# One bank's turn and one matmul's place at the change from block 1 to block 2 of a fused attention and PReLU feed-forward kernel

## The chip, the core and the metric

The kernel runs on one core of a Trainium2 chip. The metric is the device time of one execution in microseconds (us). The core's engines are named as the profile names them: PE (TensorE matmuls), PEld (its weight loads), DVE (VectorE), ACT (ScalarE), POOL (GpSimd), and SP, which only issues DMA transfers here.

## What is computed

Attention without softmax over 8 batches of 8 heads, 576 rows and 64 columns, a norm per row, and then a feed-forward layer with PReLU, all in the reference's own words:

```python
kv = np.einsum('bhsd,bhse->bhde', k, v)
out = np.einsum('bhsd,bhde->bhse', q, kv)
rms = np.sqrt(np.mean(out * out, axis=-1, keepdims=True) + 1e-06)
attn = out / rms * g_norm
x = attn.transpose(0, 2, 1, 3).reshape(4608, 512)
h = x @ w_in                                           # 512 -> 2048
g = np.maximum(h, 0.0) + alpha * np.minimum(h, 0.0)
y = g @ w_out                                          # 2048 -> 512
```

## The kernel before

The 4608 rows are worked off in 9 blocks of 512 (`w` = 0 to 8). A block's first product is cut into 16 **units** (`u` = 0 to 15), one for each 128 of the 2048 columns. A unit is `m1_group`: four matmuls of 128x512 into a PSUM bank `h_ps` (line 391), a relu of the negated bank by ACT into `m_sb` (line 398), and one operation by DVE that reads `m_sb` and the bank and writes the activation `gt` (line 402). The bank is free once that DVE operation has ended.

Which bank a unit gets is decided by `HPool` and `h_bank`: the turn `h_turn[0]` goes up by one, modulo the number of tags in `h_tags[0]`, and picks the tag. There are three tags, h0, h1 and h2, and block 1 starts with the turn at 0, so its units take h1, h2, h0, h1 and so on. In block 2, after unit 0, the list of tags becomes h1 and h2 alone (line 793), for all blocks that follow; h0 is from then on a bank of the second product.

The order of work on each engine is the order in which the program names it (a manual schedule): the loop over `w` and `u` at line 781 puts behind each unit's `m1_group` a share of other work. Each engine's instructions run in that order, and a tile's bank or buffer is taken again only when the last reader of its former contents is done.

The second product of block 0 is done plainly: 16 accumulating matmuls (`y_mm`, line 416) for each of four tiles of 128 rows. Three of these are finished before block 1. The fourth, `ys[3]`, is the **held-back tile**: it sits in the bank with tag "y", and its 16 matmuls are spread over the units of block 1. `Y3_AT[u]` gives, for each unit, the first matmul and the one after the last; those before 8 were done earlier. After the 16th, `y_out` copies the bank to SBUF with ACT (line 450) and `store_rows` issues its stores (line 427), on SP's queue.

From block 2 on, the second product of the block before is done with seven products in place of eight, on quarter blocks (`prod_mm`, line 546, matmuls of 128x256): seven matmuls behind each unit. Products 1 and 2 write the tile yX, which uses the bank with tag "y"; products 6, 7 and 4 write yY in h0; products 5 and 3 write yZ. The sums of `gt` that they need come from DVE (`s_sum`, lines 496 to 502). The attention of the next block (`step_kv` at line 327, `step_ot` at 349, `step_ssq` at 365 to 375) stands behind fixed units; `regroup_pair` (line 171, ACT) puts a part of k in order, and `dma_t` (line 317, SP) transposes q by DMA.

At the boundary the order on PE, behind `m1_group` of unit 14, is: matmul 14 of the held-back tile; unit 15; matmul 15 of the held-back tile; block 2's unit 0; seven matmuls of yX; unit 1; seven of yX; the first `step_kv` of batch 3.

Of the kernel before, what the change touches and what calls it, by code (L numbers as in the profile page):

```python
# [17 lines left out]
def kernel(  # L18
# [148 lines left out]
    def regroup(b, nm, h0, h1, eng=None):  # L167
        dst = bufs[b % NBUF][nm][:, 0:TPP, h0:h1, :].rearrange("p t h d -> p h t d")
        src = stages[b, nm][:, h0:h1, :, :]
        if eng is nc.scalar:  # L170
            nc.scalar.copy(out=dst, in_=src)
        else:
            (eng or nc.vector).tensor_copy(out=dst, in_=src)
# [6 lines left out]
    def load_gated(b):  # L180
        load_rem(b, "q")
        if b == B_NAT:
            load_q(b)
        load_rem(b, "k")
        load_main(b, "k")
        if b > B_NAT:
            load_q(b)
        load_rem(b, "v")
        load_main(b, "v")
# [8 lines left out]
    def regroup_pair(b, nm, j):  # L198
        regroup(b, nm, 2 * j, 2 * j + 2, nc.scalar)
# [112 lines left out]
    def dma_t(b):  # L312
        qt = attn_p.tile([P, NPAIR, S], FP16, name="qt_all")
        for t in range(NT):
            c0, c1 = t * P, min((t + 1) * P, S)
            src = stages[b, "q"][:, t] if t < TPP else buf_of(b, "q")[0:REM, TPP]
            nc.sync.dma_start_transpose(
                out=qt[:, :, c0:c1], in_=src.rearrange("p h d -> p (h d)"),
            )
        for j in range(NPAIR):  # L320
            qts[b, j] = qt[:, j, :]
# [59 lines left out]
    h_turn = [0]  # L381
# [25 lines left out]
    def m1_group(w, g, pool=None):  # L407
        h_ps = pool[0].tile([P, W], FP32, name="h_ps", tag=pool[1]) if pool else h_bank()
        m1_mm(h_ps, w, g, range(NC))
        m1_evac(h_ps, w, g)  # L410
# [4 lines left out]
    def y_mm(y, w, a, g):  # L415
        nc.tensor.matmul(  # L416
            out=y[:], lhsT=gt_cols(w, g, a * P, (a + 1) * P), rhs=w_out_blk(g),
            start=(g == 0), stop=(g == NF - 1),
        )
# [28 lines left out]
    def y_out(y, w, a):  # L448
        y_sb = ysb_p.tile([P, D_MODEL], FP32, name="y_sb")
        nc.scalar.copy(out=y_sb[:], in_=y[:])  # L450
        store_rows(w * W + a * P, y_sb[:], 0, D_MODEL)
# [37 lines left out]
    def s_sum(w, n, k):  # L489
        lo, hi = gts[w, k], gts[w, k + KQ]  # L490
        a11, a21 = lo[:, :, 0:HW], lo[:, :, HW:W]
        a12, a22 = hi[:, :, 0:HW], hi[:, :, HW:W]
        t = sum_p.tile([P, 2, HW], FP16, name=f"s{n}", tag=f"s{n}{k}", bufs=2 if n < 3 else 1)
        sums[w, n, k] = t
        if n == 1:
            nc.vector.tensor_add(out=t[:], in0=a21, in1=a22)
        elif n == 2:
            nc.vector.tensor_sub(out=t[:], in0=sums[w, 1, k][:], in1=a11)  # L498
        elif n == 3:
            nc.vector.tensor_sub(out=t[:], in0=a11, in1=a21)  # L500
        else:
            nc.vector.tensor_sub(out=t[:], in0=a12, in1=sums[w, 2, k][:])
# [20 lines left out]
    def prod_mm(w, n, i):  # L523
        a, c = divmod(i, NK)
        bank, fresh = y_bank(w, {1: "X", 2: "X", 6: "Y", 7: "Y", 4: "Y", 5: "Z", 3: "Z"}[n], a)
        cols = slice(a * P, (a + 1) * P)
        hi_cols = slice(HW + a * P, HW + (a + 1) * P)
        k, r = divmod(c, 2)
        if n == 1:
            lhs = gts[w, k][:, r, cols]  # L530
        elif n == 2:
            lhs = gts[w, k + KQ][:, r, cols]
        elif n == 4:
            lhs = gts[w, k + KQ][:, r, hi_cols]
        else:
            lhs = sums[w, {6: 2, 7: 3, 5: 1, 3: 4}[n], k][:, r, cols]
        q, rr = divmod(c, GW)
        if n == 1:
            rhs = w_out_sb[q][:, rr, 0:HC]
        elif n == 2:  # L540
            rhs = w_out_sb[q + WQ // 2][:, rr, 0:HC]
        elif n == 3:
            rhs = w_out_sb[q + WQ // 2][:, rr, HC:D_MODEL]
        else:
            rhs = wsum[{4: 4, 5: 1, 6: 2, 7: 3}[n]][:, c, :]
        nc.tensor.matmul(  # L546
            out=bank, lhsT=lhs, rhs=rhs, start=fresh, stop=(c == NK - 1), skip_group_check=True,
        )
# [12 lines left out]
    def y_read(w, what, subs=(0, 1)):  # L561
        if what == "p1":
            part[w, 1] = u_p.tile([P, 2, HC], FP32, name="p1")
            nc.scalar.copy(out=part[w, 1][:], in_=ybank[w, "X"][:])
            return
        if what in ("u2", "u3"):
            part[w, what] = u_p.tile([P, 2, HC], FP32, name=what)
            nc.vector.tensor_add(
                out=part[w, what][:], in0=ybank[w, "Y"][:], in1=part[w, 1][:]
            )  # L570
            return
        y_sb = ysb_p.tile([P, 2, HC], FP32, name="y_sb")
        if what == "c11":
            nc.scalar.copy(out=y_sb[:], in_=ybank[w, "X"][:])
        else:
            other = part[w, {"c21": 1, "c22": "u3", "c12": "u2"}[what]]
            if what == "c21":
                nc.vector.tensor_add(out=y_sb[:], in0=ybank[w, "Y"][:], in1=other[:])
            elif w < NW - 1:
                nc.vector.tensor_add(out=y_sb[:], in0=ybank[w, "Z"][:], in1=other[:])  # L580
            else:
                for a in subs:
                    nc.vector.tensor_add(
                        out=y_sb[:, a, :], in0=ybank[w, "Z", a][:], in1=other[:, a, :]
                    )
        quad_out(w, int(what[1]) - 1, int(what[2]) - 1, y_sb, subs)
# [160 lines left out]
    def unit_sums(w, u):  # L747
        for back, n, k in S_AT.get(u, ()):
            if 1 <= w + back < NW:
                s_sum(w + back, n, k)  # L750
# [13 lines left out]
    def attention(w, u):  # L764
        if w < NW:
            for what, j in (ATT_1 if w == 2 else ATT_AT).get(u, ()):
                if what == "t" and w >= B_NAT:
                    continue
                if w < B or what in ("ot", "ssq"):
                    if w == 2 and what in ("kv", "ssq"):  # L770
                        pool = Q_POOL if j % 2 == 0 else S_POOL
                        (step_kv if what == "kv" else step_ssq)(w, j, pool)
                    else:
                        ATT[what](w, j)

    REG_AT = {8 + 2 * j: (("k", j),) for j in range(NPAIR)}

    Y3_AT = [(8, 8), (8, 8), (8, 8), (8, 9), (9, 9), (9, 10), (10, 10), (10, 10), (10, 11), (11, 11), (11, 12), (12, 12), (12, 13), (13, 14), (14, 15), (15, 16)]
    REG_2 = {2 * j: (("k", j),) for j in range(NPAIR)}

    for w in range(1, NW):
        if w + 2 < B:
            load_gated(w + 2)
        for u in range(NF):
            m1_group(w, G_ORDER[u])
            if w > 1:
                unit_sums(w, u)
            if w == 1 and u == 2:
                regroup(2, "k", 0, H)
            if w == 1 and u == 3:  # L790
                dma_t(3)
            if w == 2 and u == 0:
                h_tags[0] = ("h1", "h2")
            if w > 2 and u == 0:
                y_read(w - 2, "c12")
            if w == 1:
                for i in range(*Y3_AT[u]):
                    y_mm(ys[3], 0, 3, i)
                    if i == NF - 1:
                        y_out(ys[3], 0, 3)  # L800
            else:
                for i in range(u * PER, (u + 1) * PER):
                    prod_mm(w - 1, *Y_LIST[i])
                for what in Y_READS.get(u, ()):
                    y_read(w - 1, what)
            attention(w + 1, u)
            if w == 1:
                for k in {5: (0,), 7: (1,)}.get(u, ()):
                    s_sum(1, 1, k)
                    s_sum(1, 2, k)  # L810
            if w + 2 < B:
                for nm, j in REG_AT.get(u, ()) if w > 1 else ():
                    regroup_pair(w + 2, nm, j)
                if u == 11 and w > 1:
                    dma_t(w + 2)
            if w == 2:
                for nm, j in REG_2.get(u, ()):
                    regroup_pair(3, nm, j)
                if u < 2:
                    s_sum(1, u + 1, 2)  # L820
# [48 lines left out]
```

## Time and profile before

| | |
|---|---|
| Time, median of 6 runs | 283.67 us (283.04 to 283.93) |
| Profiled execution, its own time | 283.51 us |
| Its span | 281.7 us |
| PE busy | 274.3 us (97%) |
| DVE, ACT busy | 219.7 us, 157.0 us |
| Granted PE clock | 1.00 |

The profile is one execution of the program, so its time differs a little from the median. Times in the views are counted from the start of its span, which is shorter than the device time by what lies around it. A view gives a start and a length; "x4" stands for four instructions of one form merged into one row, and what stands in brackets is the idle time of the engine ahead of the row and what ended it. Matmuls overlap: one of 128x512 is recorded with 379 ns, and the next starts 216 ns after it.

### The profile page before, as it was taken

How to read it: one execution, taken by the hardware profiler on the slowest of the kernel's cores; microseconds unless marked ns; L12 is line 12 of the kernel's file. 1: busy time of each engine (PE TensorE's matmuls, PEld its weight loads, DVE VectorE, ACT ScalarE, POOL GpSimd, SP SyncE). 2: the span in 40 equal slices, each digit the busy share in tenths (PEclk: the TensorE clock that was granted, in tenths of full speed). 3: DMA queues.
4: the chain of work that ended last, by engine and by line, in shares of the span. 5: the costliest groups of instructions: out<-in, count | busy, mean ns of one | idle time of the engine just before them, and what ended most of it. 6: DMA issues, size and time to landing. Idle time of an engine off the chain costs nothing.

```text
span 281.7 us, 4978 instructions
## 1 busy us (share of the span) xinstructions
PE 274.3 (97%) x1888; PEld 173.9 (62%) x1888; DVE 219.7 (78%) x418; ACT 157.0 (56%) x268; POOL 62.2 (22%) x85
## 2 busy tenths in 40 slices
PE   7899999999999999999999999999999999999995
PEld 3444444554666676666666666666666666666784
DVE  6569729898778878897879788878888788787872
ACT  3567447787667645664567466645554556443310
POOL 8744332740720036006300550000000000000000
PEclk9999999999999999999999999999999999999999
DMA  8999999999793369947973696330112011201223
GB/s 161 193 207 196 197 201 193 194 139 167 96 174 60 93 77 161 158 111 114 148 115 97 124 157 112 93 106 1 40 37 74 2 37 37 77 0 37 77 76 114
DMA packets 77628, 31.37 MB, mean 111 GB/s; under 512 B 45780, under 2 KB 77284, under 8 KB 77604
## 3 DMA queue, kind: packets, MB, share of 16 engines
q0 software_dynamic: 55600, 18.85, 59.0%
q1 hardware_dynamic: 21108, 11.25, 15.0%
q10 hardware_dynamic: 896, 0.95, 1.0%
q8 instruction: 15, 0.25, 0.4%
q14 instruction: 9, 0.07, 0.1%
HBM read 36.71 MB, written 9.44 MB: 164 GB/s over the span
## 4 chain that ended last, share of the span: by engine, by line
PE 84%; DMA 12%; issue 1%; POOL 1%; DVE 1%; ACT 0%; DVEq 0%; POOLq 0%
PE h_ps L391 39%; PE yY L546 15%; PE yZ L546 10%; PE yX L546 10%; DMA vst<-in_v_dram 5%; DMA w_in_sb<-in_moe_w_in_dram 5%; PE kv_ps L327 3%; PE ot_ps L349 3%; PE ssq_ps L365 2%; PE y L416 2%; DMA qst<-in_q_dram 2%; PE qt_ps L293 0%; POOL vst L136 0%; DVE xt L375 0%; DVE gt L402 0%
## 5 line engine op out<-in xcount | busy, mean ns | idle before, releaser
L391 PE MATMUL h_ps<-xt,w_in_sb 128*128 128x512 f16 x576 | 145.4, 379 | 0.7 <-DVE gt L402 0.5
L402 DVE SCALAR_TENSOR_TENSOR gt<-m_sb,beta_sb,h_ps 128x512 f16<-128x512 f32 x144 | 106.9, 746 | 40.8 <-ACT m_sb L398 39.0
L398 ACT ACTIVATE m_sb<-h_ps 128x512 f32<-128x512 f32 x144 | 86.0, 598 | 75.7 <-PE h_ps L391 61.0
L391 PEld LDWEIGHTS <-w_in_sb 128*128 128x128 f16 x576 | 54.8, 98 | 47.0 <-issue 1.7
L546 PEld LDWEIGHTS <-s 128*128 128x128 f16 x512 | 50.1, 98 | 19.3
L546 PEld LDWEIGHTS <-gt 128*128 128x128 f16 x384 | 37.6, 98 | 15.1 <-issue 0.4
L546 PE MATMUL yY<-wsum,s 128*128 128x256 f16 x256 | 36.3, 273 | 0.0
L546 PE MATMUL yX<-w_out_sb,gt 128*128 128x256 f16 x256 | 35.1, 273 | 0.1
L355 ACT ACTIVATE sq_sb<-ot_ps 128x512 f16<-128x512 f32 x36 | 21.3, 598 | 17.3 <-PE ot_ps L349 17.1
L367 ACT ACTIVATE rstd<-ssq_ps,eps_t 128x512 f32<-128x512 f32 x36 | 24.7, 690 | 9.7 <-PE ssq_ps L365 9.7
L375 DVE SCALAR_TENSOR_TENSOR xt<-ot_ps,g2col,rstd 128x512 f16<-128x512 f32 x36 | 26.5, 744 | 3.2 <-ACT rstd L367 3.2
L162 POOL DMA_DIRECT2D qsb<-in_q_dram x7 | 4.9, 699 | 78.7 <-DMA qt_all<-qsb 76.6
L153 POOL DMA_DIRECT2D qst<-in_q_dram x20 | 17.7, 916 | 1.9 <-DVE gt L402 1.9
L546 PE MATMUL yY<-wsum,gt 128*128 128x256 f16 x128 | 17.6, 273 | 0.0
L546 PE MATMUL yZ<-wsum,s 128*128 128x256 f16 x128 | 17.6, 273 | 0.0
L546 PE MATMUL yZ<-w_out_sb,s 128*128 128x256 f16 x128 | 17.6, 273 | 0.0
L416 PE MATMUL y<-w_out_sb,gt 128*128 128x512 f16 x64 | 17.0, 379 | 0.5 <-DMA w_out_sb<-in_moe_w_out_dram 0.5
L349 PE MATMUL ot_ps<-qt_all,kv_sb 128*128 128x512 f16 (+7 forms) x64 | 13.6, 286 | 0.4 <-DVE kv_sb L335 0.3
L327 PEld LDWEIGHTS <-ksb 128*128 128x128 f16 (+1 forms) x164 | 11.4, 98 | 4.2 <-DMA vst<-in_v_dram 1.1
L498 DVE TENSOR_TENSOR s<-s,gt 128x512 f16<-128x512 f16 x32 | 13.5, 421 | 0.5
L365 PE MATMUL ssq_ps<-sq_sb,mask 128*128 128x512 f16 x36 | 13.6, 379 | 0.2 <-ACT sq_sb L355 0.2
L335 DVE TENSOR_TENSOR kv_sb<-kv_ps,mask 128x128 f16<-128x128 f32 x32 | 9.1, 285 | 6.0 <-PE kv_ps L327 6.0
(66 smaller groups left out, 211.0 us busy)
## 6 DMA issues: line engine op xcount, KB each, us to landing
out_dram<-y_sb SPq DMA_DIRECT2D x19, 256.0 KB, 2.2
kst<-in_k_dram POOLq DMA_DIRECT2D x7, 512.0 KB, 7.7
vst<-in_v_dram POOLq DMA_DIRECT2D x7, 512.0 KB, 10.8
qst<-in_q_dram POOLq DMA_DIRECT2D x20, 128.0 KB, 7.0
w_out_sb<-in_moe_w_out_dram POOLq DMA_DIRECT2D x4, 512.0 KB, 15.8
out_dram<-y_sb SPq DMA_DIRECT2D x25, 64.0 KB, 3.2
w_in_sb<-in_moe_w_in_dram POOLq DMA_DIRECT2D x3, 512.0 KB, 12.0
out_dram<-y_sb SPq DMA_DIRECT2D x9, 128.0 KB, 2.1
```

Source lines behind the costliest of these rows:

```text
L153: nc.gpsimd.dma_start(out=st[:, t, :, :], in_=srcs["q"][b, :, t * P : (t + 1) * P, :].rearrange("h p d -> p h d"),)
L327: nc.tensor.matmul(out=kv_ps[:], lhsT=ks(t), rhs=vs(t), start=(t == 0), stop=(t == n_runs(b) - 1),)
L349: nc.tensor.matmul(out=ot_ps[:, n0 - w * W : n1 - w * W], lhsT=kvs[b, j][:], rhs=qts[b, j][:, n0 - b * S : n1 - b * S], start=True, stop=True,
L355: nc.scalar.activation(out=sq[:], in_=ot_ps[:], func=AF.Square)
L365: nc.tensor.matmul(out=ssq_ps[:], lhsT=mask16[:], rhs=sq[:], start=True, stop=True)
L367: nc.scalar.activation(out=rstd[:], in_=ssq_ps[:], func=AF.Abs_reciprocal_sqrt, bias=eps_t[:], scale=inv_d,)
L375: nc.vector.scalar_tensor_tensor(out=xts[w, j][:], in0=ot_ps[:], scalar=g2col[:], in1=rstd[:], op0=ALU.mult, op1=ALU.mult,)
L391: nc.tensor.matmul(out=h_ps[:], lhsT=w_in_blk(c, g), rhs=xts[w, c][:], start=(c == 0), stop=(c == NC - 1),)
L398: nc.scalar.activation(out=m_sb[:], in_=h_ps[:], func=AF.Relu, scale=-1.0)
L402: nc.vector.scalar_tensor_tensor(out=gts[w, i][:, r, :], in0=m_sb[:], scalar=beta_sb[:, g : g + 1], in1=h_ps[:], op0=ALU.mult, op1=ALU.add,)
L416: nc.tensor.matmul(out=y[:], lhsT=gt_cols(w, g, a * P, (a + 1) * P), rhs=w_out_blk(g), start=(g == 0), stop=(g == NF - 1),)
L546: nc.tensor.matmul(out=bank, lhsT=lhs, rhs=rhs, start=fresh, stop=(c == NK - 1), skip_group_check=True,)
```

## The change

Two places are changed. At unit 0 of block 2, where the list of tags becomes h1 and h2, the turn is set to 1 as well. And the last two entries of `Y3_AT` put the held-back tile's 16th matmul behind unit 14, together with the 15th, where it stood behind unit 15; the copy and the stores of `y_out` go with it.

```diff
-    Y3_AT = [(8, 8), (8, 8), (8, 8), (8, 9), (9, 9), (9, 10), (10, 10), (10, 10), (10, 11), (11, 11), (11, 12), (12, 12), (12, 13), (13, 14), (14, 15), (15, 16)]
+    Y3_AT = [(8, 8), (8, 8), (8, 8), (8, 9), (9, 9), (9, 10), (10, 10), (10, 10), (10, 11), (11, 11), (11, 12), (12, 12), (12, 13), (13, 14), (14, 16), (16, 16)]
...
             if w == 2 and u == 0:
                 h_tags[0] = ("h1", "h2")
+                h_turn[0] = 1
```

## The prediction, made before the changed kernel was run

> **What bounds the kernel now.** I read the page first. TensorE (PE) is the engine to follow:
>
> ```profile
> PE 274.3 (97%) x1888; PEld 173.9 (62%) x1888; DVE 219.7 (78%) x418; ACT 157.0 (56%) x268; POOL 62.2 (22%) x85
> ```
>
> 97% is an average, so I then asked for busy time by stretch, with the boundary between block 1 and block 2 (about 67 us) apart from what follows it:
>
> ```profile
> 66.90:69.60 2.70, 2.16 (x14) 1.17 (x12) 2.27 (x4) 2.18 (x4) 0.00 (x0) 1.00 1.13 166
> ...
> 72.00:277.00 205.00, 205.00 (x1471) 139.20 (x1470) 165.75 (x316) 112.76 (x193) 29.28 (x36) 1.00 0.57 85
> ```
>
> The columns are the stretch, its length, then PE, weight loads, DVE, ACT and POOL busy, the granted clock, DMA. After 72 us PE has no idle time in 205 us; in the 2.70 us at the boundary it has 0.54 us. A busy figure also counts the tail of a matmul, 0.16 us in which the next could have started (379 ns long, 216 ns apart). So the timeline of PE is needed, which gives starts:
>
> ```profile
> 65.92 1.03 PE L391 MATMUL h_ps<-xt,w_in_sb 128*128 128x512 f16 x4
> 66.78 0.38 PE L416 MATMUL y<-w_out_sb,gt 128*128 128x512 f16 x1
> 67.00 1.03 PE L391 MATMUL h_ps<-xt,w_in_sb 128*128 128x512 f16 x4
> 68.11 0.92 PE L546 MATMUL yX<-w_out_sb,gt 128*128 128x256 f16 x7
> 69.49 0.81 PE L391 MATMUL h_ps<-xt,w_in_sb 128*128 128x512 f16 x3 [0.46 <-DVE gt L402]
> ```
>
> Four matmuls of a unit take 0.86 us from start to next start (65.92 to 66.78); the seven of 256 columns take 0.76 (0.77 in the chain of waits). Block 2's first unit starts at 67.00, so yX could start at 67.86; it starts at 68.11, 0.25 late. The second unit could follow at 68.11 + 0.76 = 68.87; it starts at 69.49, 0.62 late. **Lost at the boundary: 0.87 us.** Comparing the spacing of all matmuls from 45 us on in the same way, I find no other spacing longer than its form's usual one by 15 ns.
>
> Who ends these two waits is in the timelines of ACT and DVE:
>
> ```profile
> 65.90 0.60 ACT L398 ACTIVATE m_sb<-h_ps 128x512 f32<-128x512 f32 x1
> 66.98 0.60 ACT L398 ACTIVATE m_sb<-h_ps 128x512 f32<-128x512 f32 x1 [0.48 <-PE h_ps L391]
> 67.48 0.58 ACT L450 COPY y_sb<-y 128x512 f32<-128x512 f32 x1
> 68.06 0.60 ACT L398 ACTIVATE m_sb<-h_ps 128x512 f32<-128x512 f32 x1
> 68.56 0.61 ACT L171 COPY ksb<-kst 128x512 f16<-128x512 f16 x1
> ```
>
> ```profile
> 66.78 1.58 DVE L402 SCALAR_TENSOR_TENSOR gt<-m_sb,beta_sb,h_ps 128x512 f16<-128x512 f32 x2
> 68.69 0.75 DVE L402 SCALAR_TENSOR_TENSOR gt<-m_sb,beta_sb,h_ps 128x512 f16<-128x512 f32 x1 [0.33 <-ACT m_sb L398]
> 69.36 0.75 DVE L496 TENSOR_TENSOR s<-gt 128x512 f16<-128x512 f16 x2
> ```
>
> The held-back tile's copy (L450) ends at 68.06 and frees bank "y"; yX starts 0.05 later. The first unit's evacuation (relu 68.06 to 68.66, gt 68.69 to 69.44) frees h2; the second unit starts 0.05 later, because it was given h2 again. The chain of waits goes through this pair:
>
> ```profile
> 67.16 0.88 PE h_ps L391 x4
> 68.04 0.02 issue
> 68.06 0.60 ACT m_sb L398
> 68.67 0.03 issue
> 68.69 0.76 DVE gt L402
> 69.45 0.04 issue
> 69.49 1.02 PE h_ps L391 x4
> ```
>
> **The change part by part.** *The bank.* The rotation adds 1 and takes the remainder. In block 1, unit 0 gets h1, so unit 15 gets h1, and block 2's unit 0 gets h2 with the turn left at 2. With two tags, (2+1)%2=1 is h2 again; with the turn set to 1, (1+1)%2=0 is h1. From there the banks alternate in the opposite order to before in blocks 2 to 8. No instruction is added or removed. The second unit now waits for block 1's last gt instead of block 2's first, which in this trace ends at 68.36 (66.78 + 1.58) instead of 69.44. By itself this part lets the unit start where PE is ready, 68.87: it is worth 0.62.
>
> *The held-back tile.* Its 16th matmul goes from behind unit 15's four to ahead of them; the number of matmuls before 67.00 is the same, so block 2's first unit stays at 67.00. The tile's last matmul then starts at 65.92 and ends at 66.30. The copy follows the relu of 65.90: ACT starts the next instruction 0.10 before the last one's recorded end (66.98 relu of 0.60, copy at 67.48), so it runs about 66.40 to 66.98. Bank y is free 0.88 before yX wants it at 67.86. By itself this part would gain nothing: yX would start earlier, but the second unit would still stand behind the gt of 69.44. With the other bank it is worth the 0.25.
>
> *What the move delays.* Unit 15 starts at 66.14 instead of 65.92 (one matmul, 0.216). Its relu goes from 66.98 to 67.20, ending 67.80; its gt from 67.61 to about 67.83, ending 68.58; the bank h1 is usable 0.05 later, at 68.63. PE is ready for the second unit at 67.86 + 0.76 = 68.62. The two meet within 0.01. So I take the second unit's start at 68.63, against 69.49: **0.86 us earlier**. It can't be below nothing here: DVE finishes block 1's last gt before block 2's first, which is what the unit waits for now.
>
> On the order of ACT's work the Trainium skill speaks against the change (PSUM — Partial Sum Buffer, Engine vs sequencer instructions): ScalarE's queue is strictly first in, first out, so a copy that waits also holds the relu behind it. By that rule with the copy fully in the way (0.58) the gain would be 0.28; by the rows, where the copy is over 0.22 before the relu can start, it is 0.86.
>
> The unsure part is the order on ACT, where copy and relu of unit 15 change places. If the copy were late by its whole 0.58 and held the relu of unit 15 as long, the gain would be 0.86 - 0.58 = 0.28: my lower end of this term. The upper end is the whole 0.87, since there is no third gap.
>
> *SP.* The tile's two stores leave SP at 70.03, behind the five transposes that keep it until 69.94. An earlier copy doesn't move them; had SP been free they would go out 1.1 earlier, which no instruction waits for. No POOL instruction is moved past.
>
> *What hides at no cost.* DVE's gt of the first unit needs its relu (68.66) and finds DVE free at 68.58: 0.1 to spare; if it ran late, the third unit, which needs that bank at about 70.53, has 1 us of cover. The two s of 69.36 end at 70.11, and the second unit's gt now wants DVE at 70.32 (71.18 less 0.86). The s that the yY weight load at 72.85 needs ends at 72.80; both follow that gt, so they move together. The first k, v and transposed q of batch 3 had landed by about 65, 68.3 and 71.1, and are now wanted at 70.3 and 73.8. For batch 4 the transposed q lands at 102.5, wanted at 103.5, and its issue follows a store that follows PE, so that margin of 1 us moves too. Hence nothing is late next, and 205 us of gapless PE carry 0.86 to the end.
>
> **Sum.** Profiled execution: 283.51 - 0.86 = 282.65, span 281.7 to 280.8. The median of the six runs, 283.67, is 0.16 above that execution: 283.67 - 0.86 = **282.8**, or -0.30%. About 0.2%, 0.57 us, is what a measurement of this kernel can tell from no change.
>
> **The rivals.**
> 1. *The last gt of block 1 becomes the wait.* For it: PE and the bank meet within 0.01. Against it: ACT has 0.22 between copy and relu. Each 0.1 that this gt is late costs 0.1; with the bound above, 283.67 - 0.28 = 283.4. Chance 0.12.
> 2. *Given back later.* Work whose time doesn't follow PE, such as the POOL loads for batch 4 (released by the transposes at 71.07), starts PE waiting where PE now comes 0.86 sooner. For it: the s that yY needs has 0.05 to spare. Against it: the other margins named are 1 us and more. At worst all 0.86 goes: 283.7. Chance 0.09.
> 3. *Slower: the granted clock.* With the last gaps gone PE runs from 45 to 278 us without a pause. If the clock granted after 72 us fell, 1% of 205 us costs 2.05: 282.8 + 2.05 = 284.9. It decides from 0.42% (0.86/205). For it: only that the stream gets denser. Against it: 205 us gapless at 1.00 already. Chance 0.06.
> 4. *The change doesn't do what it says*: a bank order other than the one I worked out, so the second unit still stands behind the first's gt. Then 283.7. Against it: the code fixes it. Chance 0.02.
>
> **How the numbers follow.** My forecast keeps 0.71. Faster by over 0.2% are the forecast and a part of rival 1 (late by under 0.29): 0.74. Within 0.2%: the rest of rival 1, rivals 2 and 4, and a part of the forecast that the scatter of runs (283.04 to 283.93) hides: 0.19. Slower: rival 3 and a little scatter: 0.07. The range goes down to the full 0.87 and 0.4 of scatter, 282.4, and up past rival 1's 283.4 to 283.5; beyond it lie rivals 2 and 3 and rival 4.
>
> **What would show it.** In the new profile: the copy L450 near 66.4; yX at 67.86 right behind the first unit; the second unit at 68.63 with no idle time named before it; the chain going from PE to PE here; PE idle time before 70 us down by 0.54; last PE end 0.86 sooner; the span near 280.8. The relu behind the copy starting later than 67.2, or a new wait of PE on DVE at 68.6, is rival 1. A spacing above the usual after 70 us is rival 2. A clock under 1.00 is rival 3. If the boundary is closed and the time is the same, my claim that PE carries the gain to the end is wrong.

## The result: 0.3% faster, and the profile after

The changed kernel takes 282.75 us, median of 22 runs (282.1 to 283.8), against 283.68 for the kernel before, median of 47 runs. The ratio is 0.9968, with a 95% interval of 0.9960 to 0.9975; the forecast, 282.8 against 283.67, is a ratio of 0.9969. The profiled execution took 282.63 us, with a span of 280.9.

The page's line of engines, and the busy time of the same boundary stretch as before (the stretch, its length, then PE, weight loads, DVE, ACT and POOL, the clock, DMA):

```profile
PE 274.0 (98%) x1888; PEld 173.6 (62%) x1888; DVE 219.8 (78%) x418; ACT 157.1 (56%) x268; POOL 62.2 (22%) x85
```

```profile
66.90:69.60 2.70, 2.70 (x19) 1.57 (x17) 2.27 (x4) 1.77 (x4) 0.00 (x0) 1.00 1.08 160
```

The number of instructions is unchanged, and the 0.54 us of PE's idle time at the boundary is gone: 2.70 busy of 2.70. PE's timeline of the changed kernel:

```profile
65.69 0.59 PE L416 MATMUL y<-w_out_sb,gt 128*128 128x512 f16 x2
66.12 1.89 PE L391 MATMUL h_ps<-xt,w_in_sb 128*128 128x512 f16 x8
67.85 0.93 PE L546 MATMUL yX<-w_out_sb,gt 128*128 128x256 f16 x7
68.62 1.02 PE L391 MATMUL h_ps<-xt,w_in_sb 128*128 128x512 f16 x4
69.48 0.93 PE L546 MATMUL yX<-w_out_sb,gt 128*128 128x256 f16 x7
```

The tile's last two matmuls stand together at 65.69. Unit 15 and block 2's first unit have become one row of eight, since nothing stands between them. yX follows at 67.85 (it was 68.11) and the second unit at 68.62 (it was 69.49), and no row names a wait. ACT and DVE at the same place:

```profile
65.89 0.60 ACT L398 ACTIVATE m_sb<-h_ps 128x512 f32<-128x512 f32 x1
66.39 0.58 ACT L450 COPY y_sb<-y 128x512 f32<-128x512 f32 x1
67.19 0.60 ACT L398 ACTIVATE m_sb<-h_ps 128x512 f32<-128x512 f32 x1 [0.22 <-PE h_ps L391]
68.05 0.60 ACT L398 ACTIVATE m_sb<-h_ps 128x512 f32<-128x512 f32 x1 [0.27 <-PE h_ps L391]
```

```profile
67.82 1.61 DVE L402 SCALAR_TENSOR_TENSOR gt<-m_sb,beta_sb,h_ps 128x512 f16<-128x512 f32 x2 [0.32 <-ACT m_sb L398]
```

The copy is over at 66.97, 0.22 before unit 15's relu can start; that relu waits for its matmuls, not for the copy. The two gt of the last DVE row belong to unit 15 and to block 2's first unit. The chain of waits, which went through ACT and DVE here, stays on PE:

```profile
65.86 0.43 PE y L416 x2
66.29 1.73 PE h_ps L391 x8
68.01 0.77 PE yX L546 x7
68.78 0.86 PE h_ps L391 x4
69.64 0.76 PE yX L546 x7
```

From the start of the second unit to the end of the last matmul, PE's timeline gives 209.03 us before and 209.03 after; from there to the end of the span, 3.21 in both. In these two profiles all that is won is won at the boundary: from the start of block 2's first unit to that of its second 2.49 us before, 1.63 after, 0.86 less.

### The profile page after: what moved, and what is told of

Same layout as the page of the kernel before. It is cut to its first block, busy times and chain, and to the rows that moved or that the text cites. A ratio compares the mean times of both kernels' runs of the same rounds, so it can differ in the third digit from the quotient of the medians.

```text
span 280.9 us, 4978 instructions
## 1 busy us (share of the span) xinstructions
PE 274.0 (98%) x1888; PEld 173.6 (62%) x1888; DVE 219.8 (78%) x418; ACT 157.1 (56%) x268; POOL 62.2 (22%) x85
## 4 chain that ended last, share of the span: by engine, by line
PE 85%; DMA 12%; issue 1%; POOL 1%; DVE 0%; ACT 0%; DVEq 0%; POOLq 0%
PE h_ps L391 39%; PE yY L546 15%; PE yZ L546 10%; PE yX L546 10%; DMA vst<-in_v_dram 5%; DMA w_in_sb<-in_moe_w_in_dram 5%; PE kv_ps L327 3%; PE ot_ps L349 3%; PE ssq_ps L365 2%; PE y L416 2%; DMA qst<-in_q_dram 2%; PE qt_ps L293 0%; POOL vst L136 0%; DVE xt L375 0%; ACT rstd L367 0%
```

## The experiments

This last distance, from the first unit's start to the second's, and the one from the second unit's start to the end of the last matmul, are what I compare: each is read off one profile, and neither holds the start of the kernel, where executions differ. The times of the runs stand beside them, each ratio against runs of the kernel before on the same chip; it is not the quotient of two medians of this table. Edits are against the changed kernel.

| Kernel | First unit to second: expected | measured | Second unit to last matmul | Median, us | Ratio (95%) |
|---|---|---|---|---|---|
| before | | 2.49 | 209.03 | 283.68 | 1 |
| changed | 1.63 | 1.63 | 209.03 | 282.75 | 0.9968 (0.9960 to 0.9975) |
| bank alone | 1.87 | 1.87 | 209.03 | 282.77 | 0.9976 (0.9966 to 0.9986) |
| tile alone | 2.4 to 2.5 | 2.49 | 209.03 | 283.50 | 1.0000 (0.9991 to 1.0009) |
| copy late | 2.08 | 2.09 | 209.04 | 283.14 | 0.9983 (0.9972 to 0.9993) |
| copy first | 2.09 | 2.12 | 209.03 | 283.21 | 0.9983 (0.9973 to 0.9993) |
| third bank | 1.62 | 1.63 | 209.66 | 282.84 | 0.9969 (0.9956 to 0.9983) |
| four more | | 1.63 | 209.90 | 283.63 | 1.0003 (0.9993 to 1.0014) |

### The bank alone

```diff
-... (12, 13), (13, 14), (14, 16), (16, 16)]
+... (12, 13), (13, 14), (14, 15), (15, 16)]
```

> Only the turn is set; the held-back tile's 16th matmul stays behind unit 15. My theory (the second unit starts at the later of two times, its bank free and PE ready): yX still waits for the copy and starts at 68.11, the second unit follows at 68.11 + 0.76 = 68.87. Gain 0.62 of the 0.87: span about 281.1, time about 283.05, ratio 0.9978. Rival, the other order of the banks in blocks 2 to 8 is what pays: the whole 0.87, time 282.8. Rival, the copy is the real stop and the bank only its shadow: no gain, second unit near 69.4.

PE's timeline of this kernel:

```profile
66.72 1.03 PE L391 MATMUL h_ps<-xt,w_in_sb 128*128 128x512 f16 x4
67.83 0.93 PE L546 MATMUL yX<-w_out_sb,gt 128*128 128x256 f16 x7
68.60 1.03 PE L391 MATMUL h_ps<-xt,w_in_sb 128*128 128x512 f16 x4
```

and the copy in ACT's:

```profile
67.20 0.58 ACT L450 COPY y_sb<-y 128x512 f32<-128x512 f32 x1
```

yX is still 0.25 late (66.72 + 0.86 = 67.58 would be in time; the copy ends at 67.20 + 0.58 = 67.78), and the second unit follows yX at once. 1.87 from unit to unit, 0.62 less than before, as expected. The interval of the ratio holds the expected 0.9978; the median of 282.77 is lower than the 283.05 that I had set, by 0.28, which is inside the runs' scatter. The rival with the order of the banks in blocks 2 to 8 falls: the rest of the stream is 209.03 in either order. So does the one that the copy is the real stop: the second unit starts at 68.60, not near 69.4.

The times of the runs can't tell this kernel from the changed one (0.9976 and 0.9968, medians 282.77 and 282.75). That the held-back tile adds to the bank rests on the profiles: 1.87 here, 1.63 with both, on an equal stream behind.

### The held-back tile alone

```diff
             if w == 2 and u == 0:
                 h_tags[0] = ("h1", "h2")
-                h_turn[0] = 1
```

> Only the tile's 16th matmul is moved behind unit 14; the second unit gets bank h2 again. My theory: copy near 66.4, yX at 67.86, but the second unit still behind the first unit's gt at 69.4 to 69.5, so PE now waits 0.87 in one place and nothing is gained: span 281.7, time 283.7, ratio 1.000. Rival, the two gaps are worth their length each: 0.25, time 283.4.

```profile
67.84 0.93 PE L546 MATMUL yX<-w_out_sb,gt 128*128 128x256 f16 x7
69.47 1.02 PE L391 MATMUL h_ps<-xt,w_in_sb 128*128 128x512 f16 x4 [0.70 <-DVE gt L402]
```

In this timeline of PE yX starts in time, and the idle time that stood ahead of it has moved behind it: the wait for gt is recorded as 0.70 instead of 0.46, and the second unit starts where it did. Ratio 1.0000. Half of the change is worth nothing by itself, and 1.87 - 1.63 = 0.24 us beside the other half.

### The copy behind the relu

```diff
-                    if i == NF - 1:
-                        y_out(ys[3], 0, 3)
+                if u == NF - 1:
+                    y_out(ys[3], 0, 3)
```

> Both parts, but the copy is put behind unit 15's relu on ACT, so only the matmul is early. My theory: relu 67.20 to 67.80, copy 67.69 to 68.27, yX at 68.32, second unit at 69.08. Gain 0.41: span about 281.3, time about 283.3, ratio 0.9986, less than with the bank alone. Rival, that the place of the matmul on PE is what counts and the copy has cover: 0.87, time 282.8.

ACT's timeline, and then PE's:

```profile
66.48 0.60 ACT L398 ACTIVATE m_sb<-h_ps 128x512 f32<-128x512 f32 x1 [0.70 <-PE h_ps L391]
66.98 0.58 ACT L450 COPY y_sb<-y 128x512 f32<-128x512 f32 x1
```

```profile
67.61 0.92 PE L546 MATMUL yX<-w_out_sb,gt 128*128 128x256 f16 x7 [0.30 <-ACT y_sb L450]
68.37 1.03 PE L391 MATMUL h_ps<-xt,w_in_sb 128*128 128x512 f16 x4
```

ACT had been idle for 0.70 before the relu, time in which the copy could have run; it stands behind it in the program and so it waits. yX stops for it, and the early matmul makes things worse than the bank alone (2.09 against 1.87), because it delays unit 15. What the tile's move needs is the early copy.

### The copy ahead of a relu that is ready

```diff
-            m1_group(w, G_ORDER[u])
+            if w == 1 and u == NF - 1:
+                h15 = h_bank()
+                m1_mm(h15, w, G_ORDER[u], range(NC))
+                y_mm(ys[3], 0, 3, NF - 1)
+                y_out(ys[3], 0, 3)
+                m1_evac(h15, w, G_ORDER[u])
+            else:
+                m1_group(w, G_ORDER[u])
```

with the tile's 16th matmul taken out of `Y3_AT`.

> The bank as in the changed kernel; the tile's 16th matmul behind unit 15 as before, but the copy ahead of unit 15's relu on ACT. This makes rival 1 of the prediction happen on purpose. My theory with ACT in strict order: copy 67.18 to 67.76, yX at 67.86 without a wait, the relu held to 67.66, gt 68.29 to 69.04, second unit at 69.09 waiting for that gt. Gain 0.40: span about 281.3, time about 283.3, ratio 0.9986. Rival, a relu whose bank is ready goes around a copy that waits: relu at 66.98, second unit at 68.62 to 68.87, time 282.8 to 283.05.

```profile
66.82 0.59 ACT L450 COPY y_sb<-y 128x512 f32<-128x512 f32 x1 [0.70 <-PE y L416]
67.30 1.09 ACT L398 ACTIVATE m_sb<-h_ps 128x512 f32<-128x512 f32 x2
```

```profile
67.48 0.93 PE L546 MATMUL yX<-w_out_sb,gt 128*128 128x256 f16 x7
68.74 1.02 PE L391 MATMUL h_ps<-xt,w_in_sb 128*128 128x512 f16 x4 [0.33 <-DVE gt L402]
```

Unit 15's matmuls ended at 66.57 here, but its relu starts at 67.30, behind the copy, on an ACT that had been idle for 0.70. Its gt frees the bank late, and PE stops ahead of the second unit for it. This is rival 1 of the prediction, made on purpose: it costs 2.12 - 1.63 = 0.49. The trace agrees with the rule of the Trainium skill that the prediction had set against the change (PSUM — Partial Sum Buffer, Engine vs sequencer instructions: ScalarE's queue is strictly first in, first out). In the changed kernel the copy holds nothing up, because it has nothing left to wait for there: the tile's last matmul ends at 66.28, and ACT comes to the copy at 66.39.

### A third bank for the second unit

```diff
-            if w == 2 and u == 0:
+            if w == 2 and u == 1:
                 h_tags[0] = ("h1", "h2")
-                h_turn[0] = 1
```

> Instead of setting the turn, the list is cut to two banks one unit later, so the second unit gets h0, whose last gt ends near 67.5 and not 68.57; the tile's matmul is early as in the changed kernel. My theory: in the changed kernel PE and the bank h1 meet without loss, so 1.1 us more of cover is worth nothing: second unit at 68.62, span 280.9, time 282.75, ratio 0.997; yY, which takes h0 near 71.6, finds it free since about 71.05. Rival 1 of the prediction: block 1's last gt holds the second unit in a part of the executions: faster than the changed kernel by 0.1 or more. Rival on the other side: yY now waits for h0, and the time is above 282.75.

From yX's start to the second unit's start it is 0.764 us here and 0.768 in the changed kernel: the meeting of PE and bank h1 costs 4 ns. So the bank with more time to spare is worth nothing. But 0.62 us were lost just behind, at a place where I had seen a margin:

```profile
69.19 0.93 PE L546 MATMUL yX<-w_out_sb,gt 128*128 128x256 f16 x7
70.58 0.38 PE L327 MATMUL kv_ps<-vst,ksb 128*128 128x128 f16 x4 [0.46 <-DMA vst<-in_v_dram]
```

The first key-value product of batch 3 waited 0.62 for v (69.19 + 0.77 = 69.96 would be in time). Was it the bank or the landing? I ran this kernel and the changed one once more:

> The version with the third bank once more, for its profile alone. If the wait for v of 0.62 us belongs to the late landing and not to the bank: v lands near 68.4 in most executions, the wait is gone, and second unit to last matmul is 209.03. If it belongs to the bank: again 209.6 or so.

> The changed kernel once more, as the partner of the next run on one chip, and for a second profile of it. My theory: first unit to second unit of block 2 1.63 us as in its first profile, second unit to the last matmul 209.03 if batch 3's v has landed by then, 209.03 plus the lateness if it hasn't; time near 282.75. What is told apart: v landed at 68.36 in the first profile of the changed kernel and at 70.54 in that of the version with the third bank, with the wish for it at 70.24 and 69.95.

It was the landing. The second profile of the third bank shows 209.03 from the second unit to the last matmul, with no wait for v and none of yY for h0; so does the second profile of the changed kernel (282.65 median of 11 runs, ratio 0.9967, 0.9955 to 0.9978). The view of v's tile `vst` gives the time from issue to landing, for the third bank's first and second profile in turn:

```profile
DMA to landing us min/median/max: 11.7/11.7/11.7
```

```profile
DMA to landing us min/median/max: 9.4/9.4/9.4
```

Over all eleven profiles of this study this load landed between 68.19 and 68.62 in eight, and at 69.44, 69.56 and 70.54 in three. Only the last was too late, by 0.62.

### The product that needs v, one unit later

```diff
+    ATT_3 = dict(ATT_AT)
+    ATT_3[2] = ATT_3.pop(1)
...
-            for what, j in (ATT_1 if w == 2 else ATT_AT).get(u, ()):
+            for what, j in (ATT_1 if w == 2 else ATT_3 if w == 3 else ATT_AT).get(u, ()):
```

> The changed kernel with the first key-value product of batch 3 put one unit later (unit 2 of block 2 in place of unit 1), so that v has some 1.6 us more to land. If late landings of v take back a part of the gain in many executions: faster than the changed kernel by 0.1 us or more on the same chip. If they are rare: the same, 282.75. Cost of the move: the yY weight load that needs the last s comes 0.28 earlier, the s 0.2 earlier, so up to 0.1 us of wait there.

282.98 us, median of 12 runs, ratio 0.9973 (0.9962 to 0.9985), against 0.9967 for the changed kernel on the same chip: no gain that can be told. In its profile the product starts at 72.30, with v landed at 69.44, and the move costs 0.03 (209.07 from the second unit to the last matmul; the longest spacing above the usual is 22 ns, at the yY matmul behind the s). What late landings cost, if anything, is too little for these runs to show. No version beat the changed kernel.

### Four matmuls more, far away

```diff
+            if w == 5 and u == 7:
+                h7 = h_bank()
+                for _ in range(4):
+                    nc.tensor.matmul(
+                        out=h7[:], lhsT=w_in_blk(0, G_ORDER[u]), rhs=xts[w, 0][:],
+                        start=True, stop=True,
+                    )
+                m1_mm(h7, w, G_ORDER[u], range(NC))
+                m1_evac(h7, w, G_ORDER[u])
+            else:
+                m1_group(w, G_ORDER[u])
```

> The changed kernel with four matmuls of 128x512 more, ahead of unit 7's own in block 5, that write the unit's bank and are overwritten (the result doesn't change). My theory, PE alone carries time from the boundary to the end: 4 x 0.216 = 0.86 is added whole: span about 281.7, time about 283.6, so the gain of the change is undone 150 us away from its place. Rival, other engines have a part in the bound (DVE 78% busy) or a later wait takes it up: less than 0.86 is added, time 282.8 to 283.4.

From the second unit to the last matmul it is 209.896 instead of 209.033: 0.86 is added by four matmuls of 0.216, the whole of it, as expected. The time is back at that of the kernel before (1.0003). Busy time by stretch of this kernel shows why nothing takes it up:

```profile
71.00:277.00 206.00, 206.00 (x1477) 139.69 (x1475) 165.86 (x316) 112.75 (x193) 29.32 (x36) 1.00 0.57 86
```

PE is busy for all of 206 us, DVE for 81% of it.

## Why the prediction was right, step by step

*The bound.* The two waits that I read off the starts, 0.25 and 0.62, were the two that the change could close, and they behaved as one chain: the bank alone gave 0.62, the tile alone nothing, both 0.86. Adding the gaps as if each were worth its length would have been wrong by 0.25 for the tile alone.

*The new times.* Worked out and measured in the profile: copy 66.40 and 66.39, unit 15's relu 67.20 and 67.19, yX 67.86 and 67.85, second unit 68.63 and 68.62. The unsure term, whether block 1's last gt becomes the wait (rival 1), came out at 4 ns. The lower bound for it, a gain of 0.28, was not far from the gain that is left when the copy does hold up the relu, in the kernel with the copy first: 2.49 - 2.12 = 0.37.

*Where luck helped.* That times counted from the start of the span agree to 0.01 is luck: block 2's first unit starts at 66.99 in this profile and at 67.31 in the second profile of the same kernel. The test is the distance from that unit to the second, 1.63 in both. Nor does PE run "from 45 to 278 us without a pause": in this profile the first key-value product of batch 2 starts at 52.85, 0.19 late by the usual spacing and 0.04 behind the landing of its v. Five of the eleven profiles have such a wait there, of 0.07 to 0.19; the profile before has none, so the search of it for a third gap couldn't find this one. It lies ahead of the boundary and has no part in the 0.86.

*To the end.* "205 us of gapless PE carry 0.86 to the end": 209.03 before and after, and four matmuls added there came through whole. The last matmul ends 0.87 sooner, 277.65 instead of 278.53; the medians differ by 0.93, and the interval of the ratio, worked out on 283.68, is 0.71 to 1.13.

*The other rivals.* The clock was 1.00 in the profile after the change, and 0.994 or more in every run of the changed kernel, so rival 3 didn't happen. Rival 2 was not seen in either profile of the changed kernel.

*What the prediction had wrong* is one margin. It took v's landing at 68.3 from one profile and set it against a use at 70.3, as 2 us of cover. The landing moves by over 2 us between the profiles (68.19 to 70.54; with the third bank from 70.54 to 68.62 in the same kernel), and the change brings the use 0.86 nearer. In one of eleven profiles v came too late. That was in the version with the third bank; a landing at 70.54 would be 0.3 late in the first profile of the changed kernel too, which uses v at 70.24, and in time for the kernel before, which uses it at 71.12. So rival 2 can happen by this estimate, at a place that I had put down as safe, though no profile of the changed kernel shows it and the medians don't either.

## What to carry to other kernels

Where one engine runs without a gap, look for its spacings above the usual rather than at its busy share: each can be worth its whole length, if the work behind it is gapless too. But two waits close together can be one chain, as here, where closing the first alone was worth nothing. When a list of banks is cut while a turn counts through it, work out by hand which bank the next tile gets. A margin against a DMA's landing is to be read from several profiles: here the landing moved by 2.35 us between profiles, while the distance from the first unit to the second was 1.63 in every profile with both parts of the change and the early copy.

## What the runs showed that I had not expected

Apart from the one late v, the scatter between the profiled executions lies ahead of the boundary. Block 2's first unit starts between 66.28 and 67.39 us in the eleven profiles, while the stream behind the second unit is 209.03 to 209.04 wherever it isn't changed or held by v, and the tail is 3.21 or 3.22. A gain of 0.2 us at a place in this stream could be told from one profile by the distance between two starts, where some ten runs can't tell it: their intervals reach 0.001 to either side, or 0.28 us.
